# Writing out the order of a kernel's opening and splitting fewer weight slices ahead of it

## The chip, the cores and the metric

One core of a Trainium2 chip. The metric is the device time of one execution in microseconds (us). A core has a matrix engine (TensorE, "PE" in the profile; "PEld" are its weight loads), a vector engine (VectorE, "DVE"), a scalar engine (ScalarE, "ACT"), a general engine (GpSimd, "POOL") and a queue that issues transfers (SyncE, "SP"). Each engine runs its own list of instructions in order and waits where an instruction needs the result of another engine.

## What is computed

```python
p_packed = softmax(p @ k.T / 8) @ v          # 8 batches x 8 heads, p: 32 x 64, k, v: 576 x 64
out      = softmax(q @ p_packed.T / 8) @ p_packed
x = out laid out as 4608 x 512
h = max(max(x @ w1, x @ w2), x @ w3)         # 512 -> 768
x = h @ w_out                                # 768 -> 512
h = x @ w_in                                 # 512 -> 2048
P = a0 + a1 h + a2 h^2 + a3 h^3
Q = 1 + |b0| |h| + |b1| h^2
result = (P / (Q + 1e-6)) @ w_out2           # 2048 -> 512
```

The weights `w1`, `w2`, `w3`, `w_out`, `w_in`, `w_out2` arrive as 64-bit floats, and everything else in 32 bits.

## The kernel before, in words

The kernel has two parts. The first part goes through four pairs of batches (`bp` = 0 to 3), the second part is the last MLP over nine blocks of 512 tokens. Only the first part matters here.

**A pair of batches** consists of four units (`u` = 0 to 3; unit `u` is head group `u // 2` of batch `u % 2`). The attention is folded into the first MLP: `out @ w` is `softmax(...) @ (p_packed @ w)`. The steps have one-letter names, which `Ahead.do` carries out:

- `S` (`s_stage`, L329): the scores of `p` against `k` on PE, the maximum on DVE, the exponential on ACT.
- `T` (`sum_stage`, `a_stage`): the sums on POOL, six transposes on PE, a copy on ACT (L368).
- `V` (`v_stage`): the product with `v` on PE. `Z` (`scale_stage`, `z_stage`): a scaling on DVE, a transpose on PE and a copy to `ppk` on ACT. `ppk` is `p_packed` of a unit.
- `m` (`m_stage`, L303): `ppk` times one slice of `w1..w3` on PE, then a split of the result into a high and a low part (`mh` on ACT, `ml` on DVE), since each later product is made of three matmuls of such parts (`mm3`).
- `s` (`s2_stage`, L267): the scores of `q`, two transposes and a maximum on DVE, a subtraction on POOL; after a `yield` the exponential on ACT, the sum on DVE, the scaling on POOL; after a second `yield` a transpose on DVE and a split into `a2h` (ACT) and `a2l` (POOL). `g` carries each unit that is under way over its next `yield`.
- `L`, `l`, `W`, `P` load `k`, `q`, `v` and `p`; `R` loads a raw weight slice.

**The y stage** (`y_stage`, L447): for each of six column blocks `f` and both batches of the pair, three groups of 12 matmuls (`w` = 0 to 2) on `mh`, `ml`, `a2h`, `a2l`; the maximum over the three is taken by ACT (copy) and DVE (L461), and split into `hh`, `hl`. After each group `between()` (L540) is called; it is called 36 times for a pair (`t` = 0 to 35). It carries on what runs beside: the packing of the next pair (`PACK`, steps `S` to `Z`), the `m` of the next `f`, and half a step of the weight splits. **The x2 stage** (L468) then multiplies with `w_out`, eight times for a pair, and `SECOND` (the `m0`, `m1` and the `s` steps of the next pair) runs beside it.

**The weights** are split by `decode` (L68), led by `Feed`. A raw slice (64-bit) is loaded (L100); `start` takes two operations on DVE (L76 and L78, or L80) and two on ACT (L81, L82); `finish` two more on DVE (L85, L87), for `w_out` a third (L92) and a copy, and a product on POOL (L95). There are 12 slices of `w1..w3` (each finished slice is also stored, L199, to be loaded again for later pairs) and then 4 pieces of `w_out`. `half_step` does a `start` or a `finish`. Three raw slices fit at a time.

**The order.** The text of the kernel is not its order: a planner at build time simulates the program and puts on each engine, and on SP, the instruction that can go first in its simulation; where several can, the text's order counts. So all splits, loads and stages of the opening (`START`, L507, which packs pair 0) and of the y stages may be moved ahead of what the text has before them.

Of the kernel before, what the change touches and what calls it, by code (L numbers as in the profile page):

```python
# [33 lines left out]
def attn_moe_moe2_kernel(  # L34
# [13 lines left out]
    nc = tc.nc  # L48
# [16 lines left out]
    act.preload_act_table_set("natural_log_exp_and_others")  # L65
    wide = w123.dtype != F32

    def decode(pl, raw, n, single):  # L68

        hw, lw = raw[:, :, 1], raw[:, :, 0].bitcast(U32)
        t = pl.tile([128, 768], I32, name="dec_t", bufs=2)[:, :n]
        r = pl.tile([128, 768], I32, name="dec_r", bufs=1)[:, :n]
        keep = 0x7FF00000 if single else 0x7FFFFE00
        dve.tensor_scalar(out=t, in0=hw, scalar1=keep, scalar2=None, op0=ALU.bitwise_and)  # L76
        if single:
            dve.tensor_scalar(out=r, in0=hw, scalar1=0xFFFFF, scalar2=0x100000, op0=ALU.bitwise_and, op1=ALU.bitwise_or)  # L78
        else:
            dve.tensor_scalar(out=r, in0=hw, scalar1=0x1FF, scalar2=None, op0=ALU.bitwise_and)  # L80
        act.activation(t, t, AF.Relu, scale=8.0, bias=reb)  # L81
        act.activation(r.bitcast(F32), r, AF.Copy, scale=2.0**-20)  # L82
        hi, lo = yield
        rf = lo if single else r.bitcast(F32)
        dve.scalar_tensor_tensor(out=rf, in0=lw, scalar=2.0**-52, in1=r.bitcast(F32), op0=ALU.mult, op1=ALU.add)  # L85
        hib = hi if hi is not None and hi.dtype == I32 else t
        dve.scalar_tensor_tensor(out=hib, in0=hw, scalar=-0x80000000, in1=t, op0=ALU.bitwise_and, op1=ALU.bitwise_or)  # L87
        if single:
            w = t
        else:  # L90
            w = hw
            dve.tensor_scalar(out=w, in0=hib, scalar1=-0x00800000, scalar2=None, op0=ALU.bitwise_and)  # L92
            if hib is t:
                act.copy(hi, t.bitcast(F32))
        pool.tensor_tensor(out=lo, in0=rf, in1=w.bitcast(F32), op=ALU.mult)  # L95
# [7 lines left out]
    class Feed:  # L103

        def __init__(self, pl, pieces, bufs, first=0):
            self.pl, self.pieces, self.bufs, self.raw, self.half = pl, iter(pieces), bufs, [], []
            for _ in range(first):
                self.load()  # L110
# [6 lines left out]
        def start(self):  # L117
            if self.raw:
                raw, piece = self.raw.pop(0)
                gen = decode(self.pl, raw, raw.shape[1], piece[3]) if wide else None  # L120
                if gen is not None:
                    next(gen)
                self.half.append((gen, raw, piece))

        def finish(self):
            if self.half:
                gen, raw, (tiles, _, then, single) = self.half.pop(0)
                hi, lo = tiles()
                if gen is not None:
                    try:  # L130
                        gen.send((hi, lo))
                    except StopIteration:
                        pass
                elif single:
                    act.copy(lo, raw)
                else:
                    split(hi, lo, raw, lo_eng="pool")
                if then is not None:
                    then()
                self.load()  # L140

        def half_step(self):
            if self.half:
                self.finish()
            else:
                self.start()

# [96 lines left out]
    def place(u):  # L244

        bp, g, b2 = u // 4, u // 2 % 2, u % 2
        return 2 * bp + b2, g

    def load_unit(src, u):

        t = kp.tile([128, 4 * 288], F32, name="kt", bufs=NKT)
        nc.sync.dma_start(t, src[place(u)])
        return t

    a2p = rstack.enter_context(tc.tile_pool(name="a2p", bufs=1, side="right"))
# [11 lines left out]
    def s2_stage(u, qt, done):  # L267
# [25 lines left out]
        dve.transpose(t1, t0f)  # L293
        ah = a2p.tile([128, S], F32R, name=f"a2h{g}{b2}")
        al = a2p.tile([128, S], F32R, name=f"a2l{g}{b2}")
        split(ah, al, t1, lo_eng="pool")
        done[b2][g] = ah, al

    def m_tiles(f):
# [3 lines left out]
    def m_stage(bp, g, mt):  # L303

        ps = ps_t.tile([128, 2, 512], F32, name="pst")
        wt, n = next_wt()
        for b2 in range(2):
            for h in range(4):  # L310
                i, j = divmod(h, 2)
                l, c = slice(64 * j, 64 * j + 64), 32 * (h ^ b2)
                pe.matmul(ps[c : c + 32, b2, :384], lhsT=ppk[l, bp % 2, 2 * g + b2, 32 * h : 32 * h + 32],  # L313
                          rhs=wt[l, 384 * i : 384 * i + 384], start=True, stop=True)
        again(n)
        split(*(t[:, :, g, :] for t in mt), ps[:, :, :384])


    def load_p(bp):
# [72 lines left out]
    class Ahead:  # L392
# [8 lines left out]
        def do(self, what):  # L401
            k, i = what[0], int(what[1]) if what[1:] else 0
            u = 4 * self.bp + i
            if k == "F":
                feed.half_step()
            elif k == "R":
                feed.load()
            elif k == "P":
# [17 lines left out]
            elif k == "s":  # L426
                self.soft.append(s2_stage(u, self.qt.pop(i), self.a2))
                next(self.soft[-1])
            elif k == "g":
                for y in list(self.soft):  # L430
                    if next(y, True):
                        self.soft.remove(y)
            elif k == "m":
                if i == 0:
                    self.mt = m_tiles(0)
                m_stage(self.bp, i, self.mt)

        def steps(self, text):
            for step in text.split("|"):
# [55 lines left out]
    PACK = spread(34, [(f"{k}{u}", 7 * u + d) for u in range(4) for k, d in (("S", 0), ("T", 5), ("V", 8), ("Z", 10))]  # L495
                  + [("L2", 1), ("L3", 8), ("W2", 9), ("W3", 16), ("l0", 15), ("l2", 22), ("l1", 27), ("l3", 30)])

    SECOND = "m0 s0|m1 g s2|g s1|g s3|g|g||"

    wo = list(wo_pieces())  # L500
    ws = [w_piece(f, g) for f in range(6) for g in range(2)]
    pieces = ws + wo
    ahead = Ahead(0)
    feed = Feed(wp, pieces, NRAW)
    for x in "P L0 L1 W0 R W1 L2 L3 R".split():
        ahead.do(x)
    START = ("S0|S1|T0|T1|V0 W2|Z0 F|V1 l0 W3|Z1 F|S2 l2|S3 l1|m0 F|T2 l3|T3 R|F V2|Z2|s0|V3|g Z3|s2 F|g m1|s1|g s3 F")  # L507
    for _ in ahead.steps(START):
        pass
    pool.memset(cln[:, 0:1], QC * 2.0**-64)  # L510
    pool.memset(cln[:, 1:2], -LN64)
    feed2 = None
# [1 line left out]
    y_steps = {1: range(1, 36, 4), 2: range(1, 36, 4), 3: range(1, 32, 4)}  # L514
    windows = (), (0, 2, 4, 6), (1, 3, 5)
    for bp in range(NBP):
        turn = itertools.count()
        if bp == 1:
            feed2 = Feed(wp, w2_pieces(), NRAW, NRAW)
        if bp == NBP - 1:  # L520

            nc.sync.dma_start(av, a_in.partition_broadcast(128))
            nc.sync.dma_start(bv, b_in.partition_broadcast(128))
            dve.tensor_scalar(out=babs, in0=bv, scalar1=-1.0, scalar2=None, op0=ALU.mult)
            dve.tensor_tensor(out=babs, in0=babs, in1=bv, op=ALU.max)
        now = ahead
        a2, mt = ahead.a2, ahead.mt
        hs = [[None] * 6, [None] * 6]
        if bp + 1 < NBP:
            ahead = Ahead(bp + 1)  # L530
            for x in "P L0 W0 L1 W1".split():
                ahead.do(x)
            pack = ahead.steps(PACK)
        else:
            pack = iter(())
        for f in range(6):
# [2 lines left out]

            def between(bp=bp, f=f, now=now):  # L540
                t = next(turn)
                if now.soft:
                    now.do("g")
                if f < 5 and t % 6 in (2, 4):
                    m_stage(bp, t % 6 // 2 - 1, nmt)
                if t >= 2:
                    next(pack, None)
                if bp == 0:
                    if t % 3 < 2 and t < 32:
                        feed.half_step()  # L550
                elif t in y_steps[bp]:
                    feed2.step()

            if bp == NBP - 1 and f == 2:
                load_w2(wi_at(0), 0, 1)
# [179 lines left out]
```

## Time and profile before

| | us |
|---|---|
| median of 3 runs | 1391.98 (1390.89 to 1392.49) |
| the profiled execution, time | 1393.72 |
| the profiled execution, span of the core | 1391.8 |
| PE busy in the span | 1313.8 (94%) |
| DVE busy | 1051.1 (76%) |
| ACT busy | 802.2 (58%) |
| POOL busy | 242.7 (17%) |

The profile is of one execution. Its span is from the first to the last instruction; its time is 1.9 us more. Times in the rows below are microseconds from the start of the span. PEclk is the share of TensorE's full clock that was granted in a stretch (1.00 is 2.4 GHz, 0.50 is 1.2 GHz). What stands in square brackets behind an instruction is how long its engine had been idle before it, and what ended that.

### The profile page before, as it was taken

Reading aid. Unit: us, or ns where it says so; the run is one execution under the profiler, and the core shown is the slowest. Engines: PE = TensorE matmul, PEld = TensorE weight load, DVE = VectorE, ACT = ScalarE, POOL = GpSimd, SP = SyncE. Lnnn points to the kernel's source line nnn. Section 1 sums busy time; section 2 is a strip of 40 time slices with the busy share of each in tenths; the row PEclk is TensorE's granted clock in tenths of the full one; section 3 lists DMA queues with packets and bytes.
Section 4 is the critical chain, followed back from the end, with each engine's and each line's share of the span. In section 5 each row is a group of like instructions: output and inputs, shape, how many; then the busy total and the mean of one; then the engine's idle time right before and its main releaser. Section 6 shows DMA issues by size and latency. Waiting matters only on the chain.

```text
span 1391.8 us, 21572 instructions
## 1 busy us (share of the span) xinstructions
PE 1313.8 (94%) x8496; PEld 1091.5 (78%) x8496; DVE 1051.1 (76%) x1630; ACT 802.2 (58%) x1337; POOL 242.7 (17%) x230
## 2 busy tenths in 40 slices
PE   4479899998999899999999999999999999999998
PEld 1267788878878789978888888888888888888886
DVE  5877845767677765178888988888888888888887
ACT  3444523543443333176766867768677686776765
POOL 3542242425333533000100101001010010100000
PEclk9589899999999999999999999999999999999999
DMA  9945544677464721970100101001001010010000
GB/s 307 308 138 167 158 144 145 213 230 245 155 209 156 237 93 55 325 278 1 47 14 1 61 1 38 23 0 62 0 25 37 0 54 0 16 38 1 31 0 31
DMA packets 51557, 140.86 MB, mean 101 GB/s; under 512 B 5632, under 2 KB 5632, under 8 KB 50688
## 3 DMA queue, kind: packets, MB, share of 16 engines
q1 hardware_dynamic: 51168, 138.96, 30.0%
q8 instruction: 67, 1.10, 0.3%
q10 hardware_dynamic: 288, 0.52, 0.1%
q14 instruction: 34, 0.28, 0.1%
HBM read 99.09 MB, written 40.37 MB: 100 GB/s over the span
## 4 chain that ended last, share of the span: by engine, by line
PE 81%; DVE 5%; DMA 4%; ACT 2%; issue 1%; POOL 1%; SPq 0%; ACTq 0%; POOLq 0%; DVEq 0%
PE po L61 10%; PE po L62 9%; PE po L63 9%; PE psh L62 9%; PE psh L61 9%; PE psh L63 9%; PE psy L61 8%; PE psy L62 7%; PE psy L63 7%; PE pst L313 2%; DMA wi_b<-w_scr 1%; DMA w_raw<-in_w_dram 1%; DMA x_scr<-hm 1%; PE pst L378 1%; DVE wt L87 1%
## 5 line engine op out<-in xcount | busy, mean ns | idle before, releaser
L61 PE MATMUL po<-wq_b,gh 128*128 128x512 f32 x540 | 212.3, 393 | 0.8 <-ACT gh L54 0.8
L62 PE MATMUL po<-wq_b,gh 128*128 128x512 f32 x540 | 211.3, 391 | 0.0
L62 PE MATMUL psh<-xl,wi_b 128*128 128x512 f32 x540 | 211.0, 391 | 0.0
L63 PE MATMUL psh<-xh,wi_b 128*128 128x512 f32 x540 | 210.6, 390 | 0.0
L61 PE MATMUL psh<-xh,wi_b 128*128 128x512 f32 x540 | 210.6, 390 | 0.0
L634 ACT ACTIVATE hb<-psh,babs 128x512 f32<-128x512 f32 (+1 forms) x145 | 100.2, 691 | 188.8 <-PE psh L63 188.8
L61 PE MATMUL psy<-a2h,mh 128*128 128x288 f32 x576 | 181.6, 316 | 17.1 <-DVE hm L461 8.1
L63 PE MATMUL po<-wq_b,gl 128*128 128x512 f32 x540 | 181.7, 391 | 0.0
L637 DVE SCALAR_TENSOR_TENSOR hb<-h,babs,hb 128x512 f32<-128x512 f32 (+1 forms) x145 | 108.2, 746 | 97.1 <-ACT h L635 97.0
L62 PE MATMUL psy<-a2l,mh 128*128 128x288 f32 x576 | 172.7, 300 | 4.4 <-POOL a2l L58 4.4
L63 PE MATMUL psy<-a2h,ml 128*128 128x288 f32 x576 | 172.0, 299 | 0.0
L58 POOL TENSOR_TENSOR xl<-xr,xh 128x512 fp32r<-128x512 f32 x28 | 36.6, 1306 | 633.5 <-ACT xh L54 633.5
L61 PEld LDWEIGHTS psy<-a2h,mh 128*128 128x128 f32 x576 | 110.3, 192 | 44.4 <-issue 12.9
L61 PE MATMUL psy<-hh,wo_h 128*128 128x288 f32 x384 | 117.2, 305 | 12.1 <-ACT hm L477 11.7
L63 PEld LDWEIGHTS po<-wq_b,gl 128*128 128x128 f32 x540 | 101.3, 188 | 24.0
L461 DVE TENSOR_TENSOR hm<-psy,hm 128x576 f32<-128x576 f32 x96 | 72.4, 754 | 63.2 <-PE psy L63 60.3
L61 PEld LDWEIGHTS po<-wq_b,gh 128*128 128x128 f32 x540 | 101.4, 188 | 22.9 <-ACT gh L54 1.2
L62 PEld LDWEIGHTS po<-wq_b,gh 128*128 128x128 f32 x540 | 101.4, 188 | 22.4
L61 PEld LDWEIGHTS psh<-xh,wi_b 128*128 128x128 f32 x540 | 101.4, 188 | 22.1
L62 PEld LDWEIGHTS psh<-xl,wi_b 128*128 128x128 f32 x540 | 101.4, 188 | 21.7
L63 PEld LDWEIGHTS psh<-xh,wi_b 128*128 128x128 f32 x540 | 101.4, 188 | 21.7
L62 PE MATMUL psy<-hl,wo_h 128*128 128x288 f32 x384 | 115.5, 301 | 0.0
(104 smaller groups left out, 2816.0 us busy)
## 6 DMA issues: line engine op xcount, KB each, us to landing
w_raw<-in_w_dram SPq DMA_DIRECT2D x32, 512.0 KB, 4.7
w_scr<-wt SPq DMA_DIRECT2D x32, 512.0 KB, 3.3
wt<-w_scr SPq DMA_DIRECT2D x36, 384.0 KB, 4.0
kt<-in_k_dram SPq DMA_DIRECT2D x16, 576.0 KB, 6.2
vraw<-in_v_dram SPq DMA_DIRECT2D x16, 576.0 KB, 6.5
w_raw<-in_w_dram SPq DMA_DIRECT2D x12, 768.0 KB, 12.0
kt<-in_q_dram SPq DMA_DIRECT2D x16, 576.0 KB, 6.2
x_scr<-hm SPq DMA_DIRECT2D x32, 288.0 KB, 3.3
```

Of the source, the lines that this page charges most:

```text
L58: e.tensor_tensor(out=lo, in0=src, in1=hi.bitcast(F32), op=ALU.subtract)
L61: pe.matmul(out_ap, lhsT=lh, rhs=rh, start=first, stop=False)
L62: pe.matmul(out_ap, lhsT=lh, rhs=rl, start=False, stop=False)
L63: pe.matmul(out_ap, lhsT=ll, rhs=rh, start=False, stop=last)
L87: dve.scalar_tensor_tensor(out=hib, in0=hw, scalar=-0x80000000, in1=t, op0=ALU.bitwise_and, op1=ALU.bitwise_or)
L313: pe.matmul(ps[c : c + 32, b2, :384], lhsT=ppk[l, bp % 2, 2 * g + b2, 32 * h : 32 * h + 32], rhs=wt[l, 384 * i : 384 * i + 384], start=Tru ...
L378: pe.matmul(pv[32 * h : 32 * h + 32, :64], lhsT=at[:, 3 * i + cp, o : o + 32], rhs=vt[:, h, c, :], start=c == 0, stop=c == VC - 1)
L461: dve.tensor_tensor(out=hm, in0=ps[:, :, :288], in1=hm, op=ALU.max)
L634: act.activation(hb, h, AF.Abs, scale=babs[:, 0:1])
L637: dve.scalar_tensor_tensor(out=hb, in0=h2, scalar=babs[:, 1:2], in1=hb, op0=ALU.mult, op1=ALU.add)
```

## The change

1. `START` stands under `manual_schedule`: every engine and SP keep the order of the text up to the first y stage. Its text is new. Eight half steps of the splits stand in it (four slices of `w1..w3` are split there), and the raw slices are loaded by `R` steps of their own (`half_step(False)` doesn't load).
2. From the first y stage on the planner orders again, but in pair 0 the first DVE operation of each `start` (L76) and of each `finish` (L85) is kept behind everything that the text has before it on DVE (`pin`). The half steps run at `t % 3 < 2` up to `t` = 28 (before: up to 31).
3. In `START` the low part `a2l` of the four units comes from DVE (before: POOL).
4. `m_stage` makes `mh` at once and hands back the subtraction for `ml`, which the next call of `between()` (or the new step `n`) carries out. In `between()` the half step, then `PACK`, then `m` now follow each other; before it was `m`, `PACK`, half step.
5. `finish` loads the next raw slice ahead of the store of the finished one. The loads `P L0 W0 L1 W1` of the next pair are queued behind the last load of a unit (`issue_after`). The loads of `a` and `b` for the second part, and the first operation on `b`, keep their place in the text (last pair).

```diff
+        ins = dve.tensor_scalar(out=t, in0=hw, scalar1=keep, scalar2=None, op0=ALU.bitwise_and)
+        if pin:
+            tc.keep_in_program_order(ins)
...
+        ins = dve.scalar_tensor_tensor(out=rf, in0=lw, scalar=2.0**-52, in1=r.bitcast(F32), op0=ALU.mult, op1=ALU.add)
+        if pin:
+            tc.keep_in_program_order(ins)
...
-        def finish(self):
+        def finish(self, load=True):
...
+                if load:
+                    self.load()
                 if then is not None:
                     then()
-                self.load()
...
-        split(ah, al, t1, lo_eng="pool")
+        split(ah, al, t1, lo_eng="dve" if u < 4 else "pool")
...
-        split(*(t[:, :, g, :] for t in mt), ps[:, :, :384])
+        hi, lo = (t[:, :, g, :] for t in mt)
+        act.copy(hi, ps[:, :, :384])
+        return lambda: dve.tensor_tensor(out=lo, in0=ps[:, :, :384], in1=hi.bitcast(F32), op=ALU.subtract)
...
-                feed.half_step()
+                feed.half_step(False)
...
-    SECOND = "m0 s0|m1 g s2|g s1|g s3|g|g||"
+    SECOND = "m0 s0|n m1 g s2|n g s1|g s3|g|g||"
...
+    order = ExitStack()
+    order.enter_context(tc.manual_schedule())
     feed = Feed(wp, pieces, NRAW)
-    for x in "P L0 L1 W0 R W1 L2 L3 R".split():
+    for x in "P L0 R L1 W0 R W1 L2 R L3".split():
         ahead.do(x)
-    START = ("S0|S1|T0|T1|V0 W2|Z0 F|V1 l0 W3|Z1 F|S2 l2|S3 l1|m0 F|T2 l3|T3 R|F V2|Z2|s0|V3|g Z3|s2 F|g m1|s1|g s3 F")
+    START = ("S0|F|S1|T0 F|V0 W2|Z0 T1|F|V1 W3|F Z1|S2 l0|m0 F|T2 n l2|S3|F R|V2 l1|T3 l3|Z2 V3 R|Z3|s0|m1|g s2|F n|g s1|F g|s3 R|g")
     for _ in ahead.steps(START):
         pass
+    order.close()
+    feed.pin = True
...
-            nc.sync.dma_start(av, a_in.partition_broadcast(128))
-            nc.sync.dma_start(bv, b_in.partition_broadcast(128))
+            for t, src in ((av, a_in), (bv, b_in)):
+                tc.keep_in_program_order(nc.sync.dma_start(t, src.partition_broadcast(128)))
...
-            for x in "P L0 W0 L1 W1".split():
-                ahead.do(x)
+            with tc.issue_after(last_load[0].ins):
+                for x in "P L0 W0 L1 W1".split():
+                    ahead.do(x)
...
                 t = next(turn)
+                while low:
+                    low.pop()()
                 if now.soft:
                     now.do("g")
-                if f < 5 and t % 6 in (2, 4):
-                    m_stage(bp, t % 6 // 2 - 1, nmt)
-                if t >= 2:
-                    next(pack, None)
                 if bp == 0:
-                    if t % 3 < 2 and t < 32:
+                    if t % 3 < 2 and t < 29:
                         feed.half_step()
                 elif t in y_steps[bp]:
                     feed2.step()
+                if t >= 2:
+                    next(pack, None)
+                if f < 5 and t % 6 in (2, 4):
+                    low.append(m_stage(bp, t % 6 // 2 - 1, nmt))
```

## Rows read from the trace of the kernel before

**Rows 1.** Busy us of each engine by stretch: PE, PEld, DVE, ACT, POOL; then PEclk, DMA share, GB/s

```profile
20.00:40.00 20.00, 12.18 (x178) 5.89 (x163) 16.37 (x32) 9.46 (x20) 11.05 (x14) 0.76 1.03 331
...
60.00:80.00 20.00, 9.54 (x65) 6.83 (x65) 19.48 (x28) 9.17 (x12) 14.87 (x9) 0.63 0.63 215
...
140.00:160.00 20.00, 17.13 (x130) 14.87 (x131) 17.72 (x28) 12.48 (x21) 4.90 (x6) 0.75 0.54 175
...
450.00:500.00 50.00, 43.67 (x337) 41.94 (x336) 32.82 (x51) 17.89 (x28) 22.32 (x17) 0.93 0.55 186
```

**Rows 2.** Instructions in order of time: where the y and x2 stages begin

```profile
71.71 0.61 PE L62 MATMUL psy<-a2l,mh 128*128 128x288 f32 x1 [3.15 <-POOL a2l L58]
...
83.80 0.61 PE L62 MATMUL psy<-a2l,mh 128*128 128x288 f32 x1 [1.25 <-POOL a2l L58]
...
172.20 0.40 PE L61 MATMUL psy<-hh,wo_h 128*128 128x288 f32 x1
...
215.75 0.30 PE L61 MATMUL psy<-a2h,mh 128*128 128x288 f32 x1
...
298.68 0.40 PE L61 MATMUL psy<-hh,wo_h 128*128 128x288 f32 x1
```

**Rows 3.** The same view: the chain of packing a unit (S, T, V, Z)

```profile
6.12 1.22 PE L337 MATMUL psy<-kt,pt 64*32 64x288 f32 x16 [6.12 <-DMA kt<-in_k_dram]
...
9.35 0.49 ACT L349 ACTIVATE e<-psy,mx 128x288 f32<-128x288 f32 x1
...
10.19 1.21 PE L337 MATMUL psy<-kt,pt 64*32 64x288 f32 x16 [2.86 <-DMA kt<-in_k_dram]
...
12.89 0.80 ACT L368 COPY at<-pst 96x768 f32<-96x768 f32 x1 [2.96 <-PE pst L367]
...
22.88 1.10 PE L378 MATMUL pst<-vraw,at 96*32 96x64 f32 x38
...
26.43 0.26 ACT L390 COPY ppk<-pst 128x128 f32<-128x128 f32 x1
```

**Rows 4.** The same view: an s step with little beside it, to its second product

```profile
184.07 0.72 PE L275 MATMUL psy<-kt,ppk 64*32 64x288 f32 x16
...
190.45 1.16 POOL L290 TENSOR_TENSOR e<-e,sm 128x576 f32<-128x576 f32 x1 [2.69 <-DVE sm L289]
```

**Rows 5.** Groups of DVE, 0 to 220 us: count | busy us, mean ns | idle before

```profile
L461 DVE TENSOR_TENSOR hm<-psy,hm 128x576 f32<-128x576 f32 x25 | 18.8, 752 | 10.2 <-PE psy L63 10.0 <-PE pst L389 0.2
L87 DVE SCALAR_TENSOR_TENSOR dec_t<-w_raw,dec_t 128x768 int32<-128x768 int32 x16 | 18.7, 1170 | 2.7 <-ACT dec_t L81 2.7
L58 DVE TENSOR_TENSOR ml<-pst,mh 128x768 fp32r<-128x768 f32 x16 | 15.1, 949 | 1.9 <-ACT mh L54 1.9
L76 DVE TENSOR_SCALAR dec_t<-w_raw 128x768 int32<-128x768 int32 x16 | 12.0, 748 | 8.1 <-DMA w_raw<-in_w_dram 6.2 <-POOL wt L95 1.9
L85 DVE SCALAR_TENSOR_TENSOR wt<-w_raw,dec_r 128x768 f32<-128x768 uint32 x12 | 11.5, 960 | 2.1 <-PE pst L313 2.1
L78 DVE TENSOR_SCALAR dec_r<-w_raw 128x768 int32<-128x768 int32 x12 | 10.7, 888 | 0.1
L58 DVE TENSOR_TENSOR hl<-hm,hh 128x576 fp32r<-128x576 f32 x12 | 9.0, 749 | 0.8 <-ACT hh L54 0.7
L280 DVE STREAM_TRANSPOSE e<-psy 128x288 f32<-128x288 f32 x16 | 6.8, 461 | 6.5 <-PE psy L275 6.4
L287 DVE TENSOR_REDUCE sm<-e 128x18 f32<-128x576 f32 x8 | 6.0, 748 | 8.1 <-ACT e L285 8.1
```

**Rows 6.** Groups of POOL in the same stretch

```profile
L95 POOL TENSOR_TENSOR wt<-wt,dec_t 128x768 f32<-128x768 f32 x12 | 24.3, 2022 | 23.8 <-DVE wt L85 15.8 <-issue 7.9
```

**Rows 7.** Instructions in order of time: a DVE and a POOL operation of the splits together

```profile
33.59 1.81 POOL L95 TENSOR_TENSOR wt<-wt,dec_t 128x768 f32<-128x768 f32 x1
...
34.02 1.80 DVE L78 TENSOR_SCALAR dec_r<-w_raw 128x768 int32<-128x768 int32 x1
```

**Rows 8.** Issues of transfers, the whole span: count, KB each, median us to landing

```profile
w_raw<-in_w_dram SPq DMA_DIRECT2D x12, 768.0 KB, 12.0
```

More of the change, by code (lines that the diff above doesn't have):

```diff
@@ L66, in attn_moe_moe2_kernel, with decode @@
     wide = w123.dtype != F32
-    def decode(pl, raw, n, single):
+    def decode(pl, raw, n, single, pin):
         hw, lw = raw[:, :, 1], raw[:, :, 0].bitcast(U32)
@@ L75, in decode @@
         keep = 0x7FF00000 if single else 0x7FFFFE00
-        dve.tensor_scalar(out=t, in0=hw, scalar1=keep, scalar2=None, op0=ALU.bitwise_and)
+        ins = dve.tensor_scalar(out=t, in0=hw, scalar1=keep, scalar2=None, op0=ALU.bitwise_and)
+        if pin:
+            tc.keep_in_program_order(ins)
         if single:
@@ L84, in decode @@
         rf = lo if single else r.bitcast(F32)
-        dve.scalar_tensor_tensor(out=rf, in0=lw, scalar=2.0**-52, in1=r.bitcast(F32), op0=ALU.mult, op1=ALU.add)
+        ins = dve.scalar_tensor_tensor(out=rf, in0=lw, scalar=2.0**-52, in1=r.bitcast(F32), op0=ALU.mult, op1=ALU.add)
+        if pin:
+            tc.keep_in_program_order(ins)
         hib = hi if hi is not None and hi.dtype == I32 else t
@@ L103, in attn_moe_moe2_kernel, with __init__ @@
     class Feed:
-        def __init__(self, pl, pieces, bufs, first=0):
+        def __init__(self, pl, pieces, bufs, first=0, pin=False):
+            self.pin = pin
             self.pl, self.pieces, self.bufs, self.raw, self.half = pl, iter(pieces), bufs, [], []
@@ L119, in start @@
                 raw, piece = self.raw.pop(0)
-                gen = decode(self.pl, raw, raw.shape[1], piece[3]) if wide else None
+                gen = decode(self.pl, raw, raw.shape[1], piece[3], self.pin) if wide else None
                 if gen is not None:
@@ L137, in finish, with half_step @@
                     split(hi, lo, raw, lo_eng="pool")
+                if load:
+                    self.load()
                 if then is not None:
                     then()
-                self.load()
-        def half_step(self):
+        def half_step(self, load=True):
             if self.half:
-                self.finish()
+                self.finish(load)
             else:
@@ L247, in place @@
         return 2 * bp + b2, g
+    last_load = []
     def load_unit(src, u):
         t = kp.tile([128, 4 * 288], F32, name="kt", bufs=NKT)
-        nc.sync.dma_start(t, src[place(u)])
+        last_load[:] = [nc.sync.dma_start(t, src[place(u)])]
         return t
@@ L435, in do @@
                     self.mt = m_tiles(0)
-                m_stage(self.bp, i, self.mt)
+                self.low = m_stage(self.bp, i, self.mt)
+            elif k == "n":
+                self.low()
         def steps(self, text):
@@ L516, in attn_moe_moe2_kernel @@
     for bp in range(NBP):
-        turn = itertools.count()
+        turn, low = itertools.count(), []
         if bp == 1:
@@ L520, in attn_moe_moe2_kernel @@
         if bp == NBP - 1:
-            nc.sync.dma_start(av, a_in.partition_broadcast(128))
-            nc.sync.dma_start(bv, b_in.partition_broadcast(128))
-            dve.tensor_scalar(out=babs, in0=bv, scalar1=-1.0, scalar2=None, op0=ALU.mult)
+            for t, src in ((av, a_in), (bv, b_in)):
+                tc.keep_in_program_order(nc.sync.dma_start(t, src.partition_broadcast(128)))
+            tc.keep_in_program_order(dve.tensor_scalar(out=babs, in0=bv, scalar1=-1.0, scalar2=None, op0=ALU.mult))
             dve.tensor_tensor(out=babs, in0=babs, in1=bv, op=ALU.max)
```

## The prediction

> **What bounds the kernel now.** I began with the engines' busy times by stretch. From about 100 us on PE is busy nearly throughout at full clock, and whatever shortens the work beside it there is worth little. The opening is different: from 60 to 80 us DVE is busy 19.48 of 20 us while PE does 9.54 at a clock of 0.63 [rows 1]. Then I looked for what the first y stage waits for, in the instructions by time. Batch 0 of the pair really starts when its last `a2l` comes at 71.71, batch 1 when its own comes at 83.80 [rows 2]. Both wait for POOL, and POOL for a chain whose DVE links stand in a full queue. What fills it is the groups of DVE: the splits of the raw slices (L76, L78, L85, L87) cost 0.748 + 0.888 + 0.960 + 1.170 = 3.77 us a slice [rows 5], and the planner has moved some nine of the twelve slices ahead of the start of batch 1. So the time lost lies in the opening: DVE works on slices that are needed much later, and the chain of the `s` steps waits behind them.
>
> The second thing to see is how fast a pair goes. Pair 0 needs from 83.80 to 172.20, 88.4 us, for the y stages after its first (11 of 12). Pair 1 needs from 215.75 to 298.68, 82.9 us, for all 12 [rows 2], so 11 at its rate are 76.0. The 12.4 us between are stalls in pair 0, such as the stretch from 140 to 160 us, where DVE is busy 17.72 of 20 us, PE 17.13, and the clock falls to 0.75 [rows 1].
>
> **The opening in the text's order.** I laid the new text out by hand: an engine takes its next instruction when it and the inputs are free. Durations are those of rows. A unit's scores, from the first matmul to the last exponential, take 9.84 - 6.12 = 3.7 us and some 0.1 more for reading its sum; the copy of T ends at 13.69, 3.9 later; V to `ppk` took 26.69 - 22.88 = 3.8 [rows 3].
>
> For transfers, `k` of unit 0 is there at 6.1 and of unit 1 at 10.2 [rows 3]. With the raw slice now between them, I put the first raw slice at 9, `k` of unit 1 at 11.2, `v` at 13 and the rest of the first batch by 25 (an estimate: 5.9 MB by the code's sizes, at a little under the 331 GB/s moved from 20 to 40 us [rows 1]). In that order: S0 done at 10, S1 at 15, T0's copy at 15.7, Z0 at 18.5, T1's copy at 20.6, then ACT has the second slice until 22.4 and Z1 ends at 25.5. S2 ends at 29, T2's copy at 32.2 behind the third slice, T3's at 36.6, Z3 at 39.4. So s0 begins at 39.
>
> The `s` steps: to the second product one takes 191.61 - 184.07 = 7.5 us with little beside it [rows 4], and some 2.3 more to the low part (a transpose and a subtraction on DVE at 0.75 [rows 5], a copy on ACT at 0.8 [rows 3]). Four of them are interleaved, and DVE sets their pace: two transposes of a half, two reductions and a transpose of the whole (priced as the reduction), the subtraction that is new on DVE, and some 0.5 of small ones make 2 x 0.461 + 3 x 0.748 + 0.749 + 0.5 = 4.4 us a step, 17.8 for four; with it go one and a half of a slice's halves (3.8) and one `ml` (0.95) [rows 5]: 22.5 us of DVE. Laid out with the waits in between it is 28: batch 0 is complete at 58, batch 1 at **68**. Bounds: 61 if DVE never waits; 76 if transfers are 4 us late and POOL holds DVE up. I take 68, which is 83.8 - 68.3 = **15.5 us earlier**. The first y stage lies before that point in both kernels and is hidden by the chain of batch 1.
>
> At one place the price of moving `a2l` to DVE can be disputed. Before, L78 lasted 1.80 us at 34.02 while POOL ran L95 from 33.59 [rows 7], against a mean of 0.888 [rows 5]; so DVE and POOL do hold each other up here. The Trainium skill, SBUF — State Buffer, section Who interferes with whom, says that a DVE operation with two inputs in SBUF shares a port with a GpSimd operation that reads SBUF, and the second waits for the first to end. By that rule the moved subtraction (both inputs in SBUF) could take 0.75 plus a whole POOL product beside it, some 1.2 each, 2 or 3 us for the two on the path; the row agrees in kind, for another operation. It is inside the bounds above.
>
> **The y stages of pair 0.** They get more to do on DVE, for eight slices are left for them instead of three or four. In the 36 turns there are 20 half steps: eight slices and two pieces of `w_out`. By the means: slices 8 x 3.77 = 30.1; `w_out` 2 x 4.5 (one more pass, priced as L76) = 9; maxima and `hl` of 11 y stages 11 x (2 x 0.752 + 0.749) = 24.8; ten `ml` 9.5; packing of the next pair 8 (four reductions at 0.75 and some 20 small operations, no more than 0.46 each; between 3 and 12) [rows 5]. Sum 81 us of DVE. PE alone needs 76. So this stretch is bound by DVE, just: 81 if DVE never waits, 92 if it is as full as from 140 to 160 us, 17.72 of 20 [rows 1]. The pins speak for the lower half: a maximum that frees a PSUM buffer no longer stands behind splits that belong later, which is what made 12.4 us of stalls before. I take 86, **2.4 us less** than 88.4.
>
> **What costs nothing, and its cover.** The last two `w_out` pieces now fall into the x2 stages of pair 0; they are finished two x2 stages before `m` = 2 and 3 use them, and DVE is half idle there. Without that cover one piece's chain (some 4.5 on DVE and 2.0 on POOL [rows 6]) would stand in front of PE; I put in 1 us of the 0 to 6. The split order of `m_stage` lets DVE subtract one turn later; `mh` and `ml` are wanted only at the next `f`, two turns or more on, so nothing waits. The SP changes (load ahead of store, loads of the next pair behind the last unit load, `a` and `b` late) take transfers out of the first 60 us, and nobody wants them then; behind the store in `START` (which waits for POOL) stand a raw slice and two `q`, wanted 6 us or more after they can land. In pairs 1 to 3 only the text's order changes, and the planner chooses again: stalls like that between 450 and 500 us (clock 0.93, PE 43.67 of 50 [rows 1]) may grow or shrink. I take 0 of -4 to +4.
>
> **Sum.** 1393.7 - 15.5 - 2.4 + 1 = 1376.8 for the profiled execution. That execution is 1.7 us above the median of the runs, so I predict **1375**.
>
> **Rivals.**
> *A, faster still.* The opening holds its order without contention (batch 1 at 61) and the pins let pair 0 run at pair 1's rate: -22.8 - 12.4 + 1 gives 1359.5, for the median 1358. For it: pair 1 splits weights too and runs at that rate. Against: pair 1 has less to split per turn and its `hl` on POOL. DVE's sum of 81 lies above PE's 76.
> *B, the gain is given back.* What was moved out of the opening is only paid later. If DVE is no fuller than from 140 to 160 us, the y stages take 92, and each time PE runs dry the clock drops to half, as there; with two more such drops of 20 x 0.25 = 5 us each and the opening at 68, it is -15.5 + 3.6 + 10 + 1: 1393, for the median 1391. For it: DVE's sum is 15 us above what PE's idle share leaves in the present stretch. Against: the present stretch stalls on order, not on the sum.
> *C, slower.* A pinned L76 stands in front of all later DVE work, so when its raw slice hasn't landed, the maxima and with them PE stop. Raw slices landed 12.0 us after their issue in the median [rows 8], and L76 waited 6.2 us in all for them [rows 5]. A raw slice is issued at the `finish` of the slice two ahead, five turns or some 13 us (86 / 33 a turn) before its own L76. It decides when landing takes longer than 13 us: at 16, each of the six slices after the two already loaded would stop DVE 3 us, and PE loses the same, and as much again at half its clock. That is 6 x 6 = 36 on top of the forecast's 1376.8: 1413, for the median 1411. Against: the 12.0 were measured while queues were full, in the first 80 us.
> *D, nothing happens.* If the planner's order in pair 0 stays as crowded as now, only the opening counts: 1377, which can't be told from the forecast.
>
> **How the numbers follow.** Forecast with D (median 1366 to 1386): 0.52. A: 0.20. B (1386 to 1395): 0.14, half of it within 0.2%. C: 0.14. The range leaves out half of A's far side and C: 1357 to 1394. A measurement of this kernel can tell about 0.2% (2.8 us) from no change. Faster by more: 0.52 + 0.20 + 0.05 = 0.77; within: 0.08; slower: 0.15.
>
> **What would show it.** The first batch-1 y stage near 68 us, with its `a2l` on DVE; four slices split before it, not nine. In pair 0 the idle time of PE falls on L461 without long DVE runs of split operations; the x2 stages of pair 0 begin near 154 instead of 172.2, and everything behind follows by the same shift. If the y stages begin early and the x2 stages don't, B is right; if L76 waits for transfers in the y stages, C. If pairs 1 to 3 take another length, the last term was wrong. It would be wrong altogether if the chain of the `s` steps, and not DVE, set the opening.

## The result, and the profile after

The changed kernel is slower: 1406.33 us (1401.59 to 1407.29), against 1391.43 of the kernel before, a ratio of 1.010 with an interval of 1.0076 to 1.0125. The forecast was 1375, the range 1357 to 1394. The profiled execution took 1405.68 us with a span of 1403.8, 12.0 us more than the span before.

The first matmuls of the x2 and y stages tell where the 12 us lie. First those of the changed kernel in order of time (start, duration, engine, line, operation), to be held against [rows 2]:

```profile
163.56 0.40 PE L61 MATMUL psy<-hh,wo_h 128*128 128x288 f32 x1
209.26 0.29 PE L61 MATMUL psy<-a2h,mh 128*128 128x288 f32 x1
299.72 0.40 PE L61 MATMUL psy<-hh,wo_h 128*128 128x288 f32 x1
351.58 0.29 PE L61 MATMUL psy<-a2h,mh 128*128 128x288 f32 x1
446.63 0.40 PE L61 MATMUL psy<-hh,wo_h 128*128 128x288 f32 x1
499.81 0.29 PE L61 MATMUL psy<-a2h,mh 128*128 128x288 f32 x1
606.98 0.47 PE L61 MATMUL psh<-xh,wi 128*128 128x512 f32 x1 [0.94 <-DVE hm L489]
```

and the later ones of the kernel before, which [rows 2] doesn't have:

```profile
350.31 0.30 PE L61 MATMUL psy<-a2h,mh 128*128 128x288 f32 x1
434.04 0.40 PE L61 MATMUL psy<-hh,wo_h 128*128 128x288 f32 x1
487.45 0.30 PE L61 MATMUL psy<-a2h,mh 128*128 128x288 f32 x1
594.95 0.47 PE L61 MATMUL psh<-xh,wi 128*128 128x512 f32 x1 [2.17 <-DVE hm L477]
```

The differences of neighbouring rows are the lengths of the stages:

| stage | before, us | after, us | difference |
|---|---|---|---|
| opening and y stages of pair 0 | 172.2 | 163.6 | -8.6 |
| x2 stages of pair 0 | 43.6 | 45.7 | +2.1 |
| y stages of pair 1 | 82.9 | 90.5 | +7.5 |
| x2 stages of pair 1 | 51.6 | 51.9 | +0.2 |
| y stages of pair 2 | 83.7 | 95.1 | +11.3 |
| x2 stages of pair 2 | 53.4 | 53.2 | -0.2 |
| pair 3, to the second part | 107.5 | 107.2 | -0.3 |

So the opening did gain, half of what was forecast. The loss is where the forecast put nothing: in the y stages of pairs 1 and 2, 18.8 us. The page shows the same from PE's side, in the row of the y stages' first matmuls: what PE waits for there is the maximum that frees a PSUM buffer. First before, then after (count | busy us, mean ns | idle time before, releaser):

```profile
L61 PE MATMUL psy<-a2h,mh 128*128 128x288 f32 x576 | 181.6, 316 | 17.1 <-DVE hm L461 8.1
```

```profile
L61 PE MATMUL psy<-a2h,mh 128*128 128x288 f32 x576 | 183.2, 318 | 33.7 <-DVE hm L473 18.5
```

These rows are of the whole span. The two y stages alone, first before, then after (stretch, length, busy PE, PEld, DVE, ACT, POOL with their instructions, PEclk, DMA share, GB/s):

```profile
215.75:298.68 82.93, 80.64 (x893) 67.05 (x891) 53.74 (x93) 38.23 (x71) 29.79 (x34) 1.00 0.59 187
350.31:434.04 83.73, 80.74 (x893) 67.08 (x891) 54.85 (x93) 38.22 (x71) 29.51 (x34) 1.00 0.50 162
```

```profile
209.26:299.72 90.46, 83.56 (x910) 67.69 (x909) 57.46 (x95) 38.90 (x71) 28.52 (x35) 1.00 0.57 179
351.58:446.63 95.05, 87.18 (x910) 69.73 (x908) 57.72 (x95) 38.86 (x71) 28.42 (x35) 0.96 0.45 148
```

So only half of the 18.8 us is time in which PE stands: its idle time grows from 5.3 to 14.8 us, its busy time by 9.4. Of the busy part, some 3.4 us are an estimate for a stretch of 6.8 us at half clock in pair 2 (PEclk 0.50, that is 1.2 GHz, from 379.5 to 386.3, hence the 0.96). Besides, the stage now has 192 matmuls of the `m` steps (L321) instead of 174 (L313), so a piece of the next pair's work was moved into it; what the rest consists of wasn't taken apart.

(L473 is L461 of the kernel before; other lines of `decode` and of the stages have moved too: L78 to L80, L85 to L87, L87 to L91, L92 to L96, L95 to L99, L340 to L350, L344 to L354.)

In the opening, DVE isn't crowded any more as in [rows 1]; from 20 to 40 us it is even more than half idle. The same view (PE, PEld, DVE, ACT, POOL busy, PEclk, DMA share, GB/s) after:

```profile
20.00:40.00 20.00, 12.48 (x215) 7.52 (x223) 9.04 (x20) 8.02 (x18) 5.17 (x10) 1.00 0.75 258
...
60.00:80.00 20.00, 16.05 (x97) 13.02 (x98) 16.95 (x31) 9.63 (x17) 7.30 (x9) 0.69 0.52 183
```

### The profile page after: what moved, and what is told of

It reads as the page before. It is cut to its first block, busy times and chain, and to the rows that moved or that the text cites. A ratio compares the mean times of both kernels' runs of the same rounds, so it can differ in the third digit from the quotient of the medians.

```text
span 1403.8 us, 21514 instructions
## 1 busy us (share of the span) xinstructions
PE 1319.3 (94%) x8496; PEld 1094.6 (78%) x8496; DVE 1057.5 (75%) x1634; ACT 802.6 (57%) x1337; POOL 233.3 (17%) x226
## 4 chain that ended last, share of the span: by engine, by line
PE 63%; DMA 0%; DVE 0%; issue 0%; POOL 0%; ACT 0%; POOLq 0%
PE po L61 9%; PE po L62 9%; PE po L63 9%; PE psh L62 9%; PE psh L61 9%; PE psh L63 9%; PE psy L61 2%; PE psy L62 2%; PE psy L63 2%; PE pst L321 0%; DMA w_raw<-in_w_dram 0%; DMA out_dram<-ob 0%; POOL wt L99 0%; DVE hm L489 0%; DVE hm L473 0%
## 5 line engine op out<-in xcount | busy, mean ns | idle before, releaser
L61 PE MATMUL psy<-a2h,mh 128*128 128x288 f32 x576 | 183.2, 318 | 33.7 <-DVE hm L473 18.5
L61 PEld LDWEIGHTS psy<-a2h,mh 128*128 128x128 f32 x576 | 111.2, 193 | 67.7 <-DVE hm L473 25.8
L473 DVE TENSOR_TENSOR hm<-psy,hm 128x576 f32<-128x576 f32 x96 | 72.2, 753 | 65.9 <-PE psy L63 54.6
```

The costliest lines, as they stand in the source:

```text
L61: pe.matmul(out_ap, lhsT=lh, rhs=rh, start=first, stop=False)
L473: dve.tensor_tensor(out=hm, in0=ps[:, :, :288], in1=hm, op=ALU.max)
```

## The experiments

Each kernel was measured against the kernel before on the same chip; ratios are to it. The lengths, in us, come from the first matmuls of the stages, as above.

| kernel | ratio (interval) | x2 of pair 0 begins | y of pair 1 | x2 of pair 1 | y of pair 2 | x2 of pair 2 |
|---|---|---|---|---|---|---|
| before | 1 | 172.2 | 82.9 | 51.6 | 83.7 | 53.4 |
| changed | 1.0100 (1.0076 to 1.0125) | 163.6 | 90.5 | 51.9 | 95.1 | 53.2 |
| 1 old turns in pairs 1 to 3 | 0.9997 (0.9981 to 1.0014) | 163.4 | 85.1 | 47.1 | 85.3 | 56.2 |
| 2 `ml` at once | 1.0102 (1.0072 to 1.0133) | 163.4 | 92.1 | 51.9 | 95.2 | 52.8 |
| 3 the opening alone | 1.0045 (1.0032 to 1.0059) | 174.8 | 82.9 | 51.6 | 83.7 | 53.4 |
| 4 all but the opening | 1.0107 (1.0083 to 1.0131) | 158.6 | 94.9 | 51.5 | 95.1 | 52.6 |
| 5 as 4, old turns | 0.9981 (0.9968 to 0.9993) | 159.8 | 86.4 | 47.9 | 85.3 | 57.5 |
| 6 the pins alone | 0.9946 (0.9930 to 0.9963) | 158.1 | 83.7 | 53.4 | 83.7 | 55.7 |
| 7 `m` behind PACK | 1.0095 (1.0077 to 1.0112) | 163.2 | 90.6 | 51.9 | 95.3 | 52.9 |
| 8 split step first | 1.0014 (1.0003 to 1.0025) | 160.4 | 85.2 | 49.5 | 86.8 | 55.4 |
| 9 as 1, opening planned | 0.9950 (0.9927 to 0.9973) | 156.6 | 85.2 | 49.5 | 86.7 | 54.8 |
| 10 pins in all pairs | 0.9888 (0.9874 to 0.9903) | 161.9 | 85.2 | 48.2 | 85.3 | 45.7 |
| 11 pins on the starts | 0.9913 (0.9897 to 0.9930) | 155.0 | 83.7 | 53.3 | 83.7 | 53.1 |
| 12 starts, all pairs | 0.9836 (0.9808 to 0.9863) | 156.3 | 82.9 | 47.9 | 82.9 | 51.9 |

### Which part lost: 1 to 4

Two theories stood against each other. T: the new order of the text within a turn of the y stages makes pairs 1 and 2 longer. P: the planner chooses anew behind any change of the opening, and the loss is its luck.

**1, old turns in pairs 1 to 3**, on the changed kernel:

```diff
+                if bp and f < 5 and t % 6 in (2, 4):
+                    m_stage(bp, t % 6 // 2 - 1, nmt)()
+                if bp and t >= 2:
+                    next(pack, None)
                 if bp == 0:
...
                 elif t in y_steps[bp]:
                     feed2.step()
```

> The changed kernel, but between() in pairs 1 to 3 has the order of before (m with its ml at once, then PACK, then the split step); pair 0 is untouched. Measured so far: the y stages of pair 1 and 2 went from 82.9 and 83.7 us to 90.5 and 95.1. Theory T (the order of the text within a turn did that): both come back to 83 to 85, and the kernel to 1406 - 18 = 1386 to 1390. Rival P (the planner chooses anew behind any change of the opening, and the text within a turn matters little): both stay at 88 to 96 and the kernel at 1398 to 1408.

**2, `ml` at once:** in pairs 1 to 3 the subtraction follows its `m`.

```diff
                     low.append(m_stage(bp, t % 6 // 2 - 1, nmt))
+                    if bp:
+                        low.pop()()
```

> The changed kernel, but in pairs 1 to 3 the subtraction for ml is traced right behind its m and not one turn later; the order half step, PACK, m stays. If the late ml is the cause (a PSUM buffer held one turn longer), the y stages of pairs 1 and 2 come back to 83 to 85 and the kernel to 1386 to 1390. If it is the half step ahead of PACK and m, they stay at 90 to 95 and the kernel at 1402 to 1408.

**3, the opening alone**, on the kernel before:

```diff
-    for x in "P L0 L1 W0 R W1 L2 L3 R".split():
+    order.enter_context(tc.manual_schedule())
+    for x in "P L0 R L1 W0 R W1 L2 R L3".split():
...
-        split(ah, al, t1, lo_eng="pool")
+        split(ah, al, t1, lo_eng="dve" if u < 4 else "pool")
```

(with the new `START` and the end of the manual order behind it)

> The kernel before with the opening of the changed one alone: the text's order up to the first y stage, its new text, a2l on DVE; no pins, the old order in between(), the old load and store order outside the opening, loads of the next pair free. By T the gain of the opening shows undiminished: y stages of pairs 1 and 2 at 83 to 85, kernel 1378 to 1386. If the pins are needed for the gain in pair 0, its x2 stages begin at 168 to 175 instead of 163.6 and the kernel is at 1388 to 1394. By P the y stages of pairs 1 and 2 are at 88 to 96 here too, and the kernel at 1395 to 1405.

**4, all but the opening**, on the changed kernel:

```diff
-    order.enter_context(tc.manual_schedule())
-    for x in "P L0 R L1 W0 R W1 L2 R L3".split():
+    for x in "P L0 L1 W0 R W1 L2 L3 R".split():
...
-        split(ah, al, t1, lo_eng="dve" if u < 4 else "pool")
+        split(ah, al, t1, lo_eng="pool")
```

(with the old `START`)

> All of the change but the opening: START and its loads as before, planned, a2l on POOL, t up to 31; pins, order in between(), late ml, load ahead of store and queued loads as changed. By T the loss alone: y stages of pairs 1 and 2 at 90 to 95, kernel 1392 + 18 = 1405 to 1412. By P they are anything from 83 to 95, and the kernel at 1388 to 1405.

T holds for most of the loss, and P falls. With the old turns the y stages of pairs 1 and 2 are back at 85.1 and 85.3 and the kernel at 1391.3 us, all a little above what T gave (83 to 85, 1386 to 1390); with the new turns they are 94.9 and 95.1 though the opening is the old one; with the opening alone they are 82.9 and 83.7, as before. So 3.7 of the 18.8 us are not of the turns. Kernels 5 and 9, which have the old turns too, are longer by some 5 us in these stages, and 3, which has the opening alone, isn't; so this seems to come from something else of the change (load ahead of store, queued loads, the new `SECOND`); which, wasn't tried. The late `ml` isn't it: without it they are 92.1 and 95.2.

But 3 and 4 also overturned my picture of the opening. Alone it makes the kernel slower (1397.9 us, which lies in P's range, but not for P's reason, since pairs 1 and 2 are as before), and the x2 stages of pair 0 begin 2.6 us *later* than before. Everything except the opening makes them begin at 158.6, earlier than in the changed kernel. The gain in pair 0 isn't the text's order in the opening.

### What in the turn: 7 and 8

**7, `m` behind PACK**, and **8, split step first**; both on the changed kernel, each with one half of the new order (in pairs 1 to 3; `m` with its `ml` at once):

```diff
 # 7
+                if bp and t >= 2:
+                    next(pack, None)
+                if bp and f < 5 and t % 6 in (2, 4):
+                    m_stage(bp, t % 6 // 2 - 1, nmt)()
+                if bp and t in y_steps[bp]:
+                    feed2.step()
 # 8
+                if bp and t in y_steps[bp]:
+                    feed2.step()
+                if bp and f < 5 and t % 6 in (2, 4):
+                    m_stage(bp, t % 6 // 2 - 1, nmt)()
+                if bp and t >= 2:
+                    next(pack, None)
```

> The changed kernel, but in pairs 1 to 3 a turn is PACK, m with its ml at once, split step: of the new order only m behind PACK is left. If that is what lengthens the y stages of pairs 1 and 2, they are 90 to 96 and the kernel 1401 to 1408; if it is the split step coming first, they are 83 to 87 and the kernel 1386 to 1393.

> The changed kernel, but in pairs 1 to 3 a turn is split step, m with its ml at once, PACK: of the new order only the split step coming first is left. If that is what lengthens the y stages of pairs 1 and 2 (its DVE operations are then planned ahead of the maxima of the packing and of ml), they are 90 to 96 and the kernel 1401 to 1408; if it is m behind PACK, they are 83 to 87 and the kernel 1386 to 1393.

It is `m` behind PACK: 90.6 and 95.3. The split step coming first leaves 85.2 and 86.8. Kernels 1 and 7 differ in nothing but the order of `m` and PACK, so that swap is worth 186.0 - 170.4 = 15.6 us in the two stages. What happens in such a turn is best seen in pair 1 of the changed kernel, where PE stands for 3.5 us. Instructions in order of time, those of DVE with what POOL and PE do:

```profile
231.06 0.55 PE L321 MATMUL pst<-wt,ppk 64*32 64x384 f32 x7
...
232.54 0.76 DVE L350 TENSOR_REDUCE mx<-psy 128x2 f32<-128x576 f32 x1 [1.01 <-PE pst L321]
...
233.21 0.68 DVE L91 SCALAR_TENSOR_TENSOR wt<-w_raw,dec_t 128x512 int32<-128x512 int32 x1
...
234.30 0.96 DVE L326 TENSOR_TENSOR ml<-pst,mh 128x768 fp32r<-128x768 f32 x1
235.17 0.42 DVE L96 TENSOR_SCALAR w_raw<-wt 128x512 int32<-128x512 int32 x1
235.50 0.42 DVE L76 TENSOR_SCALAR dec_t<-w_raw 128x512 int32<-128x512 int32 x1
235.72 1.34 POOL L99 TENSOR_TENSOR wt<-dec_r,w_raw 128x512 fp32r<-128x512 f32 x1 [3.98 <-DVE w_raw L96]
235.84 1.24 DVE L354 SCALAR_TENSOR_TENSOR mx<-mx 128x2 f32<-128x2 f32 x1
...
237.00 0.75 DVE L473 TENSOR_TENSOR hm<-psy,hm 128x576 f32<-128x576 f32 x1
...
237.80 0.40 PE L61 MATMUL psy<-a2h,mh 128*128 128x288 f32 x1 [3.53 <-DVE hm L473]
```

PE had finished the group at 234.3; the maximum L473 that frees its buffer is planned behind `ml` (L326), operations of two splits (L91, L96, L76) and L354, which lasts as long as POOL's product beside it. The same place in kernel 1:

```profile
234.20 0.74 DVE L350 TENSOR_REDUCE mx<-psy 128x2 f32<-128x576 f32 x1
...
235.51 0.88 PE L321 MATMUL pst<-wt,ppk 64*32 64x384 f32 x16
235.60 0.16 DVE L354 SCALAR_TENSOR_TENSOR mx<-mx 128x2 f32<-128x2 f32 x1
...
235.68 0.75 DVE L473 TENSOR_TENSOR hm<-psy,hm 128x576 f32<-128x576 f32 x1
...
236.50 0.69 DVE L91 SCALAR_TENSOR_TENSOR wt<-w_raw,dec_t 128x512 int32<-128x512 int32 x1
```

Here `m` (L321) runs after the packing's scores and not among them, its `ml` isn't ready yet, and the maximum goes first; the split follows. In pair 2 of the changed kernel the same stop comes again, behind the same operations:

```profile
378.16 1.24 DVE L354 SCALAR_TENSOR_TENSOR mx<-mx 128x2 f32<-128x2 f32 x1
...
380.12 0.61 PE L61 MATMUL psy<-a2h,mh 128*128 128x288 f32 x1 [3.53 <-DVE hm L473]
```

Kernel 7 has both stops too, of 3.53 us each, and kernel 1 has neither. These two are 7.1 of the 9.5 us by which PE stands longer. That the planner lines up the operations so because `m`'s result is ready earlier is read off this turn; for the other waits, and for the growth of the busy time, I have only the lengths of 1, 7 and 8.

### Where the gain of pair 0 comes from: 5, 6, 9 and 11

**5, as 4 with the old turns in pairs 1 to 3** (the two edits above together):

> The opening as before (planned), everything else of the change, but between() in pairs 1 to 3 has the order of before (m with its ml at once, PACK, split step). Without the new opening pair 0 reached its x2 stages at 158.6, with the old turns pairs 1 and 2 took 85.1 and 85.3. If the two add up: x2 of pair 0 at 157 to 161, y stages of pairs 1 and 2 at 83 to 87, kernel 1379 to 1385, faster than both. Rival: the planner undoes one of them when both are there, and the kernel is at 1388 to 1394.

**6, the pins alone**, on the kernel before:

```diff
+        ins = dve.tensor_scalar(out=t, in0=hw, scalar1=keep, scalar2=None, op0=ALU.bitwise_and)
+        if pin:
+            tc.keep_in_program_order(ins)
...
+        ins = dve.scalar_tensor_tensor(out=rf, in0=lw, scalar=2.0**-52, in1=r.bitcast(F32), op0=ALU.mult, op1=ALU.add)
+        if pin:
+            tc.keep_in_program_order(ins)
...
+    feed.pin = True
     pool.memset(cln[:, 0:1], QC * 2.0**-64)
```

> The kernel before with the pins alone: in pair 0, from the first y stage on, L76 and L85 of each split are kept behind what the text has before them on DVE. If it is the pins that shorten the time to the x2 stages of pair 0, by keeping the splits of the y stages out of the opening: three or four slices are stored before 62 us instead of six, batch 1 can start near 67 instead of 83.8, x2 of pair 0 at 157 to 163, pairs 1 and 2 as before (82 to 85), kernel 1378 to 1384. If the order within the turns of pair 0 (or the late ml) did it, x2 stays at 169 to 175 and the kernel at 1389 to 1395.

The pins alone are worth 7 us, 1384.5 us (1378 to 1384 expected), while the whole change cost 15. The last `a2l` of pair 0 in this kernel:

```profile
63.81 1.44 POOL L58 TENSOR_TENSOR a2l<-hm,a2h 128x576 fp32r<-128x576 f32 x1 [1.59 <-ACT a2h L54]
```

Batch 1 can start at 65.3, 18.5 us earlier than the 83.80 of [rows 2], with POOL still making `a2l` and with the old text of the opening. So the pins are enough to keep the splits of the y stages from filling DVE ahead of batch 1. Kernel 3 shows the counterpart: the opening in the text's order, but without pins. Its last two `a2l`, and the stores of the slices split meanwhile:

```profile
63.26 0.33 SPq L200 DMA_DIRECT2D w_scr<-wt  x1
67.78 0.33 SPq L200 DMA_DIRECT2D w_scr<-wt  x1
74.32 0.75 DVE L58 TENSOR_TENSOR a2l<-hm,a2h 128x576 fp32r<-128x576 f32 x1
76.76 0.33 SPq L200 DMA_DIRECT2D w_scr<-wt  x1
84.95 0.33 SPq L200 DMA_DIRECT2D w_scr<-wt  x1
87.35 0.73 DVE L58 TENSOR_TENSOR a2l<-hm,a2h 128x576 fp32r<-128x576 f32 x1
```

The first of these stores is of the fourth slice, which the opening splits itself; the other three are splits of the y stages, moved in between the steps of the opening, and batch 1 starts at 88.1.

A pin is weaker than point 2 of the change has it. It keeps an instruction behind the one that the text has just before it on DVE, and where that one is moved forward, the pinned one can go along. In the changed kernel L87 of the fifth slice, which is pinned, ran at 68.13, right behind a maximum of the first y stage (L473, at 67.52) and ahead of its own L76 at 72.77, though the text has L76 first:

```profile
68.13 1.59 DVE L87 SCALAR_TENSOR_TENSOR wt<-w_raw,dec_r 128x768 f32<-128x768 uint32 x1
...
72.77 1.01 DVE L76 TENSOR_SCALAR dec_t<-w_raw 128x768 int32<-128x768 int32 x2
```

Kernel 5 gained less than expected: 1388.6 us, not 1379 to 1385. It has the pins and the old opening, but it isn't as fast as 6; its y stages of pair 1 (86.4) and x2 stages of pair 2 (57.5) are longer by 2.7 and 1.8. The rest of the change (load ahead of store, queued loads, the turns of pair 0) thus costs some us; which part, wasn't tried.

**9, the opening planned:** kernel 1 without `manual_schedule`.

```diff
-    order.enter_context(tc.manual_schedule())
...
-    order.close()
```

> The changed kernel with the old turns in pairs 1 to 3 (as in the first experiment, 1391.3 us) and without manual_schedule: the new text of the opening is planned and not kept word for word. If it is keeping the text's order that costs, by making DVE wait in line where the planner would do something else (from 20 to 40 us it is busy 9.0 of 20 us in the changed kernel and 13 to 14 where the opening is planned with pins behind it), x2 of pair 0 begins at 156 to 161 instead of 163.4, and the kernel is at 1385 to 1389. If it is the new text itself (what is loaded and split when), it stays at 162 to 165 and 1390 to 1393.

The new text is fine; keeping its order costs. Planned, it brings x2 of pair 0 to 156.6 and the kernel to 1386.4 (kernel 1: 1391.3). From 20 to 40 us DVE, ACT and POOL all do more in kernel 9 than in the changed kernel above, and the transfers run at 368 GB/s instead of 258:

```profile
20.00:40.00 20.00, 11.29 (x130) 4.93 (x134) 13.66 (x30) 9.16 (x19) 9.67 (x13) 1.00 1.03 368
```

and its last `a2l` comes 5.2 us before that of kernel 1 (71.46):

```profile
66.25 0.75 DVE L58 TENSOR_TENSOR a2l<-hm,a2h 128x576 fp32r<-128x576 f32 x1
```

**11, pins on the starts alone** (kernel 6 without the pin on L85):

> The kernel before with the pin on the first operation of each start (L76) alone, in pair 0; the pin on L85 left out. L85 can't come before its L76, so if all that matters is that no split of the y stages starts in the opening, this does the same as both pins: x2 of pair 0 at 156 to 162, kernel 1382 to 1387. If the place of the second half counts, because finishing early delays the maxima, x2 is at 163 to 172 and the kernel at 1388 to 1393.

1380.6 us, better than both pins by 4 us (the intervals of the two ratios just touch), and x2 of pair 0 at 155.0: both a little better than the better forecast. But the reason given there doesn't hold: L85 *can* come before its L76, for it is made from L78's result and not from L76's. In kernel 11 (L87 is L85 of the kernel before, L80 its L78) three later slices have had their L80 and L87 done by 52 us, before the first of them has its L76:

```profile
32.53 1.60 DVE L87 SCALAR_TENSOR_TENSOR wt<-w_raw,dec_r 128x768 f32<-128x768 uint32 x1
...
41.78 1.54 DVE L87 SCALAR_TENSOR_TENSOR wt<-w_raw,dec_r 128x768 f32<-128x768 uint32 x1 [0.78 <-ACT dec_r L84]
...
51.01 0.90 DVE L87 SCALAR_TENSOR_TENSOR wt<-w_raw,dec_r 128x768 f32<-128x768 uint32 x1
...
60.09 0.50 DVE L76 TENSOR_SCALAR dec_t<-w_raw 128x768 int32<-128x768 int32 x1
```

In kernel 6 the first of these L87 comes at 62.95. So in 11 the splits do begin in the opening, while DVE has room, and the pin holds back what hangs on L76 (the last DVE operation and POOL's product). Batch 1 starts later than in 6, at 67.7 instead of 65.3, but the way from there to the x2 stages is 87 us instead of 93: less of the splits is left for it. That this is where the 4 us come from is argued from these times; no run tests it.

### A version that beats both: 10 and 12

**10, pins in all pairs**, and **12, pins on the starts in all pairs** (kernels 6 and 11 with this line more):

```diff
             feed2 = Feed(wp, w2_pieces(), NRAW, NRAW)
+            feed2.pin = True
```

> The kernel before with pins on all splits, those of the second MLP's weights in pairs 1 to 3 too (pair 0 alone gave 1384.5). If the stalls in the x2 stages of pairs 1 and 2 (53.4 and 55.7 us against 46.6 in pair 0) are split steps planned too early, these shorten to 46 to 50 each and the kernel comes to 1372 to 1380. If the planner had placed them well enough, or the pinned steps now wait in line for their transfers, it is at 1383 to 1390 or above.

> The kernel before with pins on the starts alone (L76), in all pairs. If the two gains found (10.9 us from the starts of pair 0, and 7.7 us more where both pins reached into pairs 1 to 3) add up: x2 of pair 0 at 153 to 158, its x2 stages and those of pairs 1 and 2 at 45 to 50, kernel 1370 to 1376. If the x2 stages of pairs 1 and 2 need the pin on the second half as well, they stay at 51 to 54 and the kernel at 1378 to 1383.

10 gives 1376.8 us and 12 gives 1369.7, a ratio of 0.9836 (0.9808 to 0.9863). In 10 the x2 stages of pair 2 fall from 55.7 us in kernel 6 to 45.7. In 6, then in 10, busy times over the same stage:

```profile
425.00:481.00 56.00, 48.02 (x416) 42.84 (x403) 42.17 (x70) 20.24 (x33) 25.84 (x19) 0.94 0.69 229
```

```profile
425.00:471.00 46.00, 45.46 (x410) 40.68 (x404) 31.40 (x56) 17.64 (x27) 21.51 (x16) 1.00 0.53 179
```

DVE had 70 operations in the stretch, 36 of them of the splits, and now has 56 with 22 of the splits; PE is busy 45.46 of 46 us at full clock. In 12 the x2 stages of pairs 1 and 2 are 47.9 and 51.9 us, the second longer than in 10 and than the 45 to 50 expected, but pair 0 and the y stages are shorter; why the second half needs its pin there, and nowhere else, stays open.

## Why the prediction was wrong

**The reading of the bottleneck was right.** DVE in the opening, filled with splits that belong later, held up batch 1. The pins alone, on the kernel before, bring the x2 stages of pair 0 forward by 14.1 us (6), and all kernels with pins, a planned opening and the old turns (5, 6, 9 to 12) are faster, by 0.2 to 1.6%.

**The step that failed most is the last line of what "costs nothing":** "In pairs 1 to 3 only the text's order changes, and the planner chooses again [...] I take 0 of -4 to +4". It was +18.8 in the y stages of pairs 1 and 2: 15.6 from `m` behind PACK (7 against 1), 3.7 from parts of the change that weren't tried one by one, and -0.5 between 7 and the changed kernel. The last sign that the prediction names, another length of pairs 1 to 3, is the one that came. I had laid out the turns of pair 0 and asked of the others only how long their stalls were, not what in a turn stands in front of the maximum. The trace of the kernel before had the means to ask: of the 82.9 us for the 12 stages of pair 1 PE was busy 80.64, so a new order there had 2.3 us to win and much to lose.

**The opening was mis-sized:** -15.5 forecast, -10.9 measured. The text's order was laid out well up to the first s step: it was forecast to begin at 39 and began at 39.80; batch 0 was complete at 61.6 instead of 58. Then, up to the start of batch 1:

```profile
59.22 1.69 DVE L80 TENSOR_SCALAR dec_r<-w_raw 128x768 int32<-128x768 int32 x1
...
68.13 1.59 DVE L87 SCALAR_TENSOR_TENSOR wt<-w_raw,dec_r 128x768 f32<-128x768 uint32 x1
...
72.10 0.74 DVE L58 TENSOR_TENSOR a2l<-hm,a2h 128x576 fp32r<-128x576 f32 x1
...
72.90 0.61 PE L62 MATMUL psy<-a2l,mh 128*128 128x288 f32 x1 [1.00 <-DVE a2l L58]
```

72.9 instead of 68.3. Two things stood in front that the layout didn't have: L80 of the fifth slice, which has no pin and was moved into the opening, and L87 of the same slice, whose pin let it go ahead as told above; 3.3 us together. So "four slices split before it" wasn't quite kept. (Two slips in that sum change nothing: four steps of 4.4 us are 17.7, not 17.8, and the 3.8 us are both halves of a slice, not one and a half.) And I credited the wrong part: what made the opening short is the pins (6), not the text's order, which costs 5 us (9 against 1).

**The y stages of pair 0 were mis-sized the other way:** from 72.9 to 163.6 is 90.7 for 11 of them; I took 86 and had 81 to 92. "The pins speak for the lower half" failed; the price by DVE's fill from 140 to 160 us (92, rival B's first term) was the better one. Its second term, two more drops of the clock, didn't come (in stretches of 20 us PEclk was 1.00 from 80 to 160 us, but for 0.91 from 120 to 140). Nor does the clock drop each time PE runs dry: after the stop of 3.53 us in pair 1 PEclk was 1.00 (237.2 to 244.0), after the like stop in pair 2 it was 0.50. The x2 stages of pair 0 took 2.1 more, 1 was forecast.

**Rival C fell:** L76 never waited for a raw slice. Groups of DVE from 0 to 220 us, after, against 6.2 us of such waits in [rows 5]:

```profile
L76 DVE TENSOR_SCALAR dec_t<-w_raw 128x768 int32<-128x768 int32 x16 | 11.0, 691 | 0.0
```

**The disputed price:** `a2l` on DVE cost its 0.74 to 0.76 in the changed kernel, where no POOL operation ran beside it. In kernel 9 one of the four did start inside POOL's L298, and it took twice as long, in the way the prediction feared:

```profile
53.27 1.16 POOL L298 TENSOR_TENSOR e<-e,sm 128x576 f32<-128x576 f32 x1 [1.31 <-DVE sm L297]
...
53.51 1.53 DVE L58 TENSOR_TENSOR a2l<-hm,a2h 128x576 fp32r<-128x576 f32 x1 [0.38 <-ACT a2h L54]
```

L354 above, too, took 1.24 us instead of 0.16, ending with POOL's L99. The Trainium skill, SBUF — State Buffer, section Who interferes with whom, says that a DVE instruction with two inputs in SBUF contends with a GpSimd instruction that reads SBUF; both pairs here are of that kind, and the traces agree, for L354 even at two columns.

**No rival had the mechanism.** The slower case should have been: a reordered turn puts ready work ahead of the maximum in stages where PE has hardly any slack.

In sum: -10.9 (batch 1) + 2.3 (y stages of pair 0) + 2.1 (x2 of pair 0) + 18.8 (y stages of pairs 1 and 2) - 0.3 (the rest) = 12.0, the difference of the spans.

## What to carry to other kernels

Where a planner fills an engine with work that is merely ready, it was enough here to hold back the *first* instruction of each late piece, so that what hangs on it stays back and the rest may still fill gaps; keeping the whole section in the text's order took away fills that did no harm. A stage in which the bottleneck engine has hardly a gap has little to win and much to lose by a new order of what runs beside it, so an edit to shared code is to be costed in every stage that calls it. And when several such edits are made at once, measure them one by one: here one was worth 7 to 11 us, one cost 5 and one cost 15.

## What the runs showed of the hardware that wasn't expected

An operation of two columns on DVE (L354) took 1.24 us instead of 0.16 when it began 0.12 us after a product on POOL; both ended within 0.02 us of each other. Of the 16 such operations in the changed kernel's trace, the two that began inside L99 (at 235.84 and 378.16) took 1.24 us and the other 14 took 0.15 or 0.16. So short operations are held up as well as long ones, and one of them at the head of DVE's queue delays all behind it.
